# Fused gated attention and low-rank mixer on one core: where the mixer's bursts and low-rank adds stand

## The chip, the cores and the metric

The kernel runs on one core of one Trainium2 chip. The metric is the device time of one execution in microseconds (us), lower is better. Engines are named as in the profile: PE (TensorE matmuls), PEld (its weight loads), DVE (VectorE), ACT (ScalarE), POOL (GpSimd), SP (SyncE, here only a DMA queue).

## The reference

B = 8 batches, S = 3136 rows, D = 256 columns, z has 64 columns, the low rank is 32, the mixer's hidden width is 1024.

```
scores = (1/S) * z @ z^T                      # S x S, symmetric
x      = u * (max(scores, 0)**2 @ v)          # gated attention, S x D
h      = x^T @ U @ V                          # low rank along the rows: (D x S) @ (S x 32) @ (32 x S)
y      = x + h^T
out    = y + max(y @ w_ch1, 0) @ w_ch2        # mixer: D -> 1024 -> D
```

All inputs and the output are float32; the kernel computes matmuls in bfloat16 with float32 accumulation.

## The kernel before

**Tiles and turns.** A batch's 3136 rows are 25 tiles of 128 rows (the last, number 24, has 64). The tiles are worked on in the order 12, 13, ..., 24, 0, ..., 11. The place of a tile in this order, 0 to 24, is called its turn here; the code's loop `for i in range(begin, NT)` counts turns. Tiles go in pairs that share accumulators: turns (0,1), (2,3), ..., (10,11), then 12 alone, then (13,14), ..., (23,24). `open_pair` gives a pair one of two PSUM sets, each of two banks `ps` (one bank for each half of the contraction, since the two 64-row halves of PE run side by side), and the sets alternate from pair to pair. `close_pair` empties the set at the end of the pair's last turn: ACT copies bank 1 (line 385), DVE adds bank 0 (386) and multiplies with `u` (395), which gives `x_bf`.

**One turn.** `attend_steps` makes 24 steps of two matmuls (line 371), one for each source tile. About half of the steps read a block of `A` (squared scores as they were computed), the others a block of `strip`, the transpose of one row of `A`, which a DMA transpose on SP's queue (line 333) fetches some turns ahead into one of five buffers. Between the steps stand the scores of later turns and of the next batch (`score`): PE (line 298), ACT's relu (311), DVE's square (313).

**The mixer of the batch before.** While batch b attends, batch b-1 goes through the mixer. At the end of turn 0 `rank_once` computes `t1 = x^T U` (line 479, DVE 490). The rows are divided into seven chunks of four tiles (chunk 3 has three, chunk 6 two), in the order of turns. For a chunk, `low_rank` adds `h^T`: up to four matmuls (line 531) into a PSUM set, two DVE adds (545), one for each bank, into `x_bf`, and a DMA transpose to `ut` on SP's queue (504; three buffers). Then `up_steps` (563: four steps of four matmuls, `w_ch1`, relu on ACT 581, in some chunks half of the steps on DVE 571 and ACT 579) and `down_steps` (610: one step of eight matmuls for each tile, `w_ch2`; for each pair of tiles a DVE add 624 and a store, on POOL's queue, in the last batch on SP's).

**Where these stand is written out by hand.** Every engine runs its instructions in the order in which the code issues them. The dict `ahead` gives the turn at which chunk c's `low_rank` is put among the attention's steps, and `at` the step; the dict `burst_at` gives the turns after which bursts of the mixer run. A burst n merges the up steps of chunk n with the down steps of chunk n-1, with the loads of the next batch's `v` between them; burst 1 also carries DVE's copies of the next `z` (`double_z`). The next `z` is transposed on SP's queue at turns 7 and 10 (`turn_z`), and DVE extends the second part at turn 11 (`extend_z`, line 238).

**PSUM outside the accumulators.** Up steps and scores take two double banks of their own. Low-rank matmuls, down steps and some up steps take a set from `spare()`:

```
def spare():
    return sets[(opened[0] + (0 if acc else 1)) % 2]
```

With a pair open (`acc` is not empty), this is the set that the next pair will open; between a pair's close and the next open, it is the set of the pair just closed.

**The last batch.** After its turns there is no attention left to run beside its own mixer. Before its loop ends, the up steps of the last chunk of batch 6 and that batch's last down steps are kept back in `late`; they fill the time in which the last batch's `rank` sums are finished. `mix` makes chunk 0's mixer input directly (DVE, line 522), and the low-rank adds of the other chunks are placed between up and down steps. In these two chunks (`alone`) every second up step takes its PSUM from `spare()` instead of the double banks.

## Time and profile before

| | us |
|---|---|
| time, median of 3 runs (lowest to highest) | 1007.39 (1005.87 to 1008.55) |
| profiled execution: its own time | 1007.39 |
| profiled execution: its span | 1005.6 |
| PE busy in the span | 984.7 |
| ACT busy | 612.2 |
| DVE busy | 550.6 |
| POOL busy | 171.7 |

The span runs from the first to the last instruction of the program; the device time is 1.8 us longer. One batch takes about 121.9 us in the trace, and batches 1 to 6 repeat each other closely, so that a row of one of them stands for six. In the rows below the columns are the start in us, the time that the group took in us, the engine, the line, the operation, what it writes and reads, shape, count, and in square brackets the idle time before it and what ended it. A row joins instructions of one kind; a matmul's own time (0.27 us for 256 columns) is longer than the pitch at which matmuls follow each other, since they are pipelined.

### The profile page before, as it was taken

What the parts mean: (1) busy time and instruction counts of PE and PEld (TensorE: products, weight loads), DVE (VectorE), ACT (ScalarE), POOL (GpSimd) and SP (SyncE); (2) the same over time, 40 slices, a digit from 0 to 9 for tenths busy, and PEclk for the clock granted to TensorE, in tenths of its full rate; (3) what the DMA queues carried; (4) which work ended last, traced back from release to release, by engine and by line L of the source; (5) the groups of instructions that cost most, each with busy time, mean ns of one, the idle gap of its engine ahead of it and who ended that gap; (6) DMA issues with size and microseconds to landing.
All of it is one profiled execution on the core that took longest, in us unless ns stands there. A gap on an engine that the chain in (4) does not pass through costs nothing.

```text
span 1005.6 us, 30980 instructions
## 1 busy us (share of the span) xinstructions
PE 984.7 (98%) x13648; PEld 776.2 (77%) x13688; DVE 550.6 (55%) x1003; ACT 612.2 (61%) x835; POOL 171.7 (17%) x317
## 2 busy tenths in 40 slices
PE   8899999999999999999999999999999999999998
PEld 6578777787778877788777887778878788777866
DVE  6868754457444664446644566445664457542352
ACT  7877764667645776456754667556674666643154
POOL 5112112111121111121112211112111120011000
PEclk9999999999999999999999999999999999999999
DMA  9999979999898998999988997989989998568542
GB/s 190 185 188 208 172 157 172 194 178 165 152 200 166 173 166 161 182 177 173 163 176 167 183 170 146 190 172 177 177 150 188 175 180 159 132 140 155 128 98 97
DMA packets 414790, 167.94 MB, mean 167 GB/s; under 512 B 389488, under 2 KB 399408, under 8 KB 414656
## 3 DMA queue, kind: packets, MB, share of 16 engines
q1 hardware_dynamic: 385424, 99.68, 61.4%
q0 software_dynamic: 29232, 66.28, 28.4%
q8 instruction: 107, 1.75, 0.7%
q14 instruction: 27, 0.22, 0.1%
HBM read 61.88 MB, written 25.69 MB: 87 GB/s over the span
## 4 chain that ended last, share of the span: by engine, by line
PE 91%; DMA 3%; ACT 3%; DVE 2%; issue 0%; POOL 0%; DVEq 0%; ACTq 0%; POOLq 0%
PE ps L371 48%; PE ps L610 17%; PE ps L563 17%; PE ps L298 6%; ACT A L311 2%; PE ps L405 1%; DMA strip<-A 1%; PE ps L531 1%; DMA zT<-z_bf 1%; DVE x_bf L545 1%; DMA z_c<-in_z_dram 1%; DVE A L313 1%; PE ps L479 1%; PE ps L462 0%; DVE o_sb L624 0%
## 5 line engine op out<-in xcount | busy, mean ns | idle before, releaser
L311 ACT ACTIVATE A<-ps 128x832 bf16<-128x832 f32 (+9 forms) x477 | 358.9, 769 | 161.6 <-PE ps L298 153.4
L371 PE MATMUL ps<-v,A 64*128 64x256 bf16 x4988 | 341.5, 270 | 5.5 <-DVE x_bf L545 3.8
L313 DVE TENSOR_TENSOR A<-A 128x832 bf16<-128x832 bf16 (+9 forms) x477 | 244.7, 526 | 142.2 <-ACT A L311 139.2
L371 PE MATMUL ps<-v,strip 64*128 64x256 bf16 x4420 | 308.9, 270 | 2.7 <-DMA strip<-A 2.6
L371 PEld LDWEIGHTS <-A 64*128 64x128 bf16 x4988 | 246.8, 94 | 52.7 <-issue 16.2
L581 ACT ACTIVATE relu_bf<-ps 128x1024 bf16<-128x1024 f32 (+2 forms) x206 | 186.2, 911 | 139.7 <-PE ps L563 138.9
L371 PEld LDWEIGHTS <-strip 64*128 64x128 bf16 x4420 | 223.5, 94 | 38.0 <-DMA strip<-A 3.5
L624 DVE TENSOR_TENSOR o_sb<-ps,x_bf 128x512 f32<-128x512 f32 (+2 forms) x105 | 69.8, 665 | 243.5 <-PE ps L610 228.3
L610 PE MATMUL ps<-w_bf,relu_bf 128*128 128x256 bf16 (+1 forms) x1600 | 201.3, 273 | 0.6 <-DVE o_sb L624 0.5
L563 PE MATMUL ps<-ut,w_bf 128*128 128x512 bf16 (+2 forms) x856 | 196.3, 352 | 2.1
L610 PEld LDWEIGHTS <-relu_bf 128*128 128x128 bf16 (+1 forms) x1600 | 152.8, 98 | 46.2 <-issue 4.5
L298 PE MATMUL ps<-zT 64*128 64x416 bf16 (+8 forms) x812 | 133.6, 312 | 0.0
L563 PEld LDWEIGHTS <-w_bf 128*128 128x128 bf16 x896 | 85.0, 98 | 61.9 <-issue 6.7
L355 POOL DMA_DIRECT2D u_sb<-in_u_dram x96 | 53.7, 559 | 456.5 <-DVE x_bf L395 441.0
L385 ACT COPY both<-ps 128x512 f32<-128x512 f32 (+1 forms) x104 | 58.9, 566 | 73.5 <-PE ps L371 65.9
L637 POOL DMA_DIRECT2D out_dram<-o_sb x84 | 46.0, 547 | 279.9 <-DVE o_sb L624 276.5
L386 DVE TENSOR_TENSOR both<-ps,both 128x512 f32<-128x512 f32 (+1 forms) x104 | 69.2, 666 | 26.5 <-ACT both L385 25.9
L395 DVE TENSOR_TENSOR x_bf<-both,u_sb 128x512 bf16<-128x512 f32 (+1 forms) x104 | 69.8, 671 | 3.7
L545 DVE TENSOR_TENSOR x_bf<-ps,x_bf 128x512 bf16<-128x512 f32 (+1 forms) x112 | 65.4, 626 | 6.4 <-PE ps L531 6.3
L298 PEld LDWEIGHTS <-zT 64*128 64x128 bf16 x812 | 45.0, 94 | 4.2
L244 POOL DMA_DIRECT2D v<-in_v_dram x61 | 34.0, 561 | 0.9 <-DMA w_bf<-in_moe_w_ch_dram 0.8
L298 PE MATMUL ps<-relu_bf 64*128 64x416 bf16 (+9 forms) x121 | 21.9, 335 | 4.1 <-ACT A L311 3.3
(54 smaller groups left out, 206.5 us busy)
## 6 DMA issues: line engine op xcount, KB each, us to landing
u_sb<-in_u_dram POOLq DMA_DIRECT2D x96, 256.0 KB, 3.9
out_dram<-o_sb POOLq DMA_DIRECT2D x84, 256.0 KB, 3.2
v<-in_v_dram POOLq DMA_DIRECT2D x57, 192.0 KB, 4.6
strip<-A SPq DMA_TRANSPOSE x196, 5.3
out_dram<-o_sb SPq DMA_DIRECT2D x11, 256.0 KB, 2.0
z_c<-in_z_dram POOLq DMA_DIRECT2D x7, 384.0 KB, 5.8
u_sb<-in_u_dram POOLq DMA_DIRECT2D x16, 64.0 KB, 2.7
ut<-x_bf SPq DMA_TRANSPOSE x56, 3.9
```

Of the source, the lines that this page charges most:

```text
L298: mm(out=ps[:, k, :n], lhsT=zT[halves[k], j, :], rhs=zT_flat[halves[k], c : c + n], start=True, stop=True,)
L311: nc.scalar.activation(out=dst, in_=src, func=AF.Relu, scale=sc)
L313: nc.vector.tensor_tensor(out=dst, in0=dst, in1=dst, op=ALU.mult)
L371: mm(out=acc[t0][h][:, (o - t0) * D : (o - t0 + 1) * D], lhsT=w[halves[h]], rhs=v_both[b % 2][halves[h], j, :], start=start, stop=stop, **kw,)
L385: nc.scalar.copy(out=both[:, :w], in_=banks[1][:, :w])
L386: nc.vector.tensor_tensor(out=both[:, :w], in0=banks[0][:, :w], in1=both[:, :w], op=ALU.add)
L395: nc.vector.tensor_tensor(out=x_at(b, t0, n), in0=split(both[:, :w]), in1=u_sb[:, :n, :].rearrange("p t (a c) -> p t a c", c=P), op=ALU.mult,)
L545: nc.vector.tensor_tensor(out=q, in0=split(ps[h][:, : len(ks) * D]), in1=q, op=ALU.add)
L563: mm(out=ps[i][:, :w] if apart else ps[:, i, :w], lhsT=w1_bf[:, db, (hp + i) * P : (hp + i + 1) * P], rhs=uT[c][:, db, len(chunks[c]) * P ...
L581: nc.scalar.activation(out=relus[c][:, hp : hp + 2, :w], in_=ps[:, :, :w], func=AF.Relu)
L610: mm(out=ps[r, k * D : (k + 1) * D], lhsT=relus[c][:, ht, q : q + (TAIL if two else P)], rhs=w2_bf[:, ht, :], start=(ht < 1 + two), stop=( ...
L624: nc.vector.tensor_tensor(out=o_sb[:p].rearrange("p t (a c) -> p t a c", c=P), in0=split(ps[:p, k0 * D : (k + 1) * D]), in1=x_at(b, t, nk) ...
```

## The change

It moves work in the program and changes no arithmetic. In every batch the mixer runs in three bursts instead of four: chunks 0 to 2 after turn 4, 3 to 5 after turn 11, 6 and the rest after turn 16 (before: after turns 4, 8, 13 and 17). The low-rank adds of chunks 0 to 6 stand in turns 1, 2, 3, 6, 7, 10 and 14 (before: 2, 3, 6, 7, 10, 11, 14), at step 17 in the first turn of a pair and in turn 1, else at step 12 (before: 17, 13 in turn 7, else 10).

In the last batch the kept-back up steps run on without a break before the rest of `rank`, one of the two kept-back down steps stands before `mix` and one after it; chunk 0's own low-rank add moves from chunk 1's burst to chunk 0's, behind its first up step, and takes its PSUM from `spare()` instead of the set `other`; chunk 2's follows the third up step instead of the second. The last pair of tiles is added and stored as one piece of 256 KB instead of two of 128 KB.

```diff
-        apart = b == B - 1 and c == NC - 1
...
-            if apart or k == len(pair) - 1:
-                k0 = k if apart else 0
-                t, nk = pair[k0], k + 1 - k0
-                if k0 == 0:
-                    hold[1] = out_pool.tile([P, 2, D], FP32, name="o_sb")
-                o_sb = hold[1][:, k0 : k + 1, :]
+            if k == len(pair) - 1:
+                t, nk = pair[0], len(pair)
+                o_sb = out_pool.tile([P, 2, D], FP32, name="o_sb")
                 p = P if t < NF else TAIL
                 nc.vector.tensor_tensor(
-                    out=o_sb[:p].rearrange("p t (a c) -> p t a c", c=P),
-                    in0=split(ps[:p, k0 * D : (k + 1) * D]),
+                    out=o_sb[:p, :nk, :].rearrange("p t (a c) -> p t a c", c=P),
+                    in0=split(ps[:p, : nk * D]),
                     in1=x_at(b, t, nk)[:p],
                     op=ALU.add,
                 )
...
-                    store(out=rows(out[b])[:, t : t + nk, :], in_=o_sb)
+                    store(out=rows(out[b])[:, t : t + nk, :], in_=o_sb[:, :nk, :])
...
-        burst_at = {4: (0, 1), 8: (2, 3), 13: (4, 5), 17: (6, 7)}
+        burst_at = {4: (0, 1, 2), 11: (3, 4, 5), 16: (6, 7)}
...
-        ahead = dict(zip((2, 3, 6, 7, 10, 11, 14), range(NC)))
+        ahead = dict(zip((1, 2, 3, 6, 7, 10, 14), range(NC)))
...
             if b and i in ahead:
-                at = 17 if (i + (i > FIRST)) % 2 == 0 else 13 if i == 7 else 10
+                at = 17 if (i + (i > FIRST)) % 2 == 0 or i == 1 else 12
                 main.insert(at, lambda c=ahead[i]: low_rank(b - 1, c))
...
     other = sets[opened[0] % 2]
-    ups = NH // 2
     rank(b, other[0], 0, NT - 3)
-    run(late[: ups // 2])
+    run(late[: NH // 2])
     rank(b, other[0], NT - 3)
-    run(late[ups // 2 : ups])
+    run(late[NH // 2 : NH // 2 + 1])
     mix(b, 0)
+    run(late[NH // 2 + 1 :])
     low_rank(b, 1, other)
-    run(late[ups:])
     for c in range(NC + 1):
         up, down = last[c]
-        steps = _merge(up, down)
-        adds = {0: ((2, 2),), 1: ((0, 1), (3, 5))}.get(c, ((c + 2, 2),) if c + 2 < NC else ())
-        for n, at in reversed(adds):
-            steps.insert(at, lambda n=n: low_rank(b, n, other, n > 0))
-        run(steps)
+        if c + 2 < NC:
+            up.insert(3 if c == 0 else 1, lambda c=c: low_rank(b, c + 2, other))
+        if c == 0:
+            up.insert(1, lambda: low_rank(b, 0, None, False))
+        run(_merge(up, down))
```

## The prediction

> **What bounds the kernel now.** I read the page first (engine shares, chain), then the waits of PE, then the timeline around each place that the change touches. The profiled execution took 1007.39 us, which is also the median of the runs, and its span is 1005.6 us, so differences of the span add straight to the median. Of this kernel a difference below 0.3% (3.0 us) can hardly be told from none.

> The page, sections 1 and 4:

> ```profile
> PE 984.7 (98%) x13648; PEld 776.2 (77%) x13688; DVE 550.6 (55%) x1003; ACT 612.2 (61%) x835; POOL 171.7 (17%) x317
> PE 91%; DMA 3%; ACT 3%; DVE 2%; issue 0%; POOL 0%; DVEq 0%; ACTq 0%; POOLq 0%
> ```

> PE is the bound nearly everywhere: 20.9 us of its span are idle, most of them in the start-up. No matmul is added or removed, so the change can only move PE's small stalls. The waits of PE name those that lie where the change works:

> ```profile
> PE ps L371 <- DVE x_bf L545: 3.8, 7, 0.5
> PE ps L610 <- DVE o_sb L624: 0.5, 1, 0.5
> ```

> The first is one stall in each of seven batches: a low-rank add (L545) on DVE still reads the PSUM set that the next pair of output tiles wants to open. The second is the last store's, once.

> **Turn 7: a stall that shrinks.** Timeline of batch 6, around the end of turn 7:

> ```profile
> 750.37 0.69 DVE L313 TENSOR_TENSOR A<-A 128x128 bf16<-128x128 bf16 x2
> ...
> 751.71 0.49 PE L371 MATMUL ps<-v,strip 64*128 64x256 bf16 x5
> ...
> 752.00 1.01 DVE L545 TENSOR_TENSOR x_bf<-ps,x_bf 128x512 bf16<-128x512 f32 x2
> ...
> 752.74 0.72 PE L371 MATMUL ps<-v,A 64*128 64x256 bf16 x5 [0.54 <-DVE x_bf L545]
> ...
> 753.07 0.22 PEld L371 LDWEIGHTS <-A 64*128 64x128 bf16 x5 [0.24 <-issue]
> ```

> The last L371 of turn 7 starts at 751.93, pairs follow each 0.11, so turn 8 was due at 752.04; its second matmul, on the other bank, starts at 753.07, just after the second add: 1.03 us lost. After: the low-rank step stands one step earlier, and in the built program it now precedes the second score of the turn, so on DVE its adds precede that score's square. They follow the squares that end at 751.06: first add then, second 0.60 later, 0.68 long, release near 752.3. It is a 4-tile chunk instead of a 3-tile one (one matmul more, due 752.1). Stall 0.2; gain 0.8 us per batch.

> **Turn 1: a new stall.** Before, no low-rank step stands here. Timeline:

> ```profile
> 720.46 0.59 DVE L313 TENSOR_TENSOR A<-A 128x832 bf16<-128x832 bf16 x1 [0.69 <-ACT A L311]
> ...
> 721.39 0.71 PE L371 MATMUL ps<-v,A 64*128 64x256 bf16 x10
> ```

> Thirteen steps of turn 1 are done at 720.02, at 0.11 each step 17 comes at 720.45. Four matmuls take 0.22, so turn 2, due at 721.39, is now due at 721.6 (the 0.22 is only moved, from turn 11). The adds wait for the square that ends at 721.06: 720.98 to 721.66 and 721.58 to 722.26, release 722.31. Turn 1 is the second of its pair, so turn 2 opens the very set that was just used: stall 0.7 us per batch. Bounds: 0.2 (if only the first bank counted) to 1.3 (both adds after another square); I take 0.7, from the rows nearest to it. Queued behind on PE are turn 2's scores; ACT and DVE behind them shift as a whole. Turn 3's step stands two steps later than before, but DVE still runs its adds after the same square: its stall of 0.2 at turn 4 stays. Turn 14's two short adds end before turn 15 in both. Turns 2, 6 and 10 are first of their pairs: nothing opens after them.

> **Turn 16: a second new stall.** The bursts stood after turns 4, 8, 13, 17, all first of a pair: the open pair holds one set, the down steps take the other, long free. Turns 11 and 16 are second of a pair: the pair has just closed, and `spare()` gives the set it closed in. The first down step writes bank 1, which ScalarE must first copy (L385). At the end of turn 16:

> ```profile
> 804.43 0.86 ACT L311 ACTIVATE A<-ps 128x832 bf16<-128x832 f32 x1 [0.19 <-PE ps L298]
> ...
> 805.20 0.58 ACT L385 COPY both<-ps 128x512 f32<-128x512 f32 x1
> ```

> L385 stands behind a score's relu and ends at 805.78. The last L371 of the turn starts at 804.45, the burst would start 0.2 later (see below), its first up step is 256 wide (4 x 0.11), so the down step is due at 805.09 and starts at 805.83: 0.74 us. In the last batch there is no score and no up step; the copy takes 0.58 from some 0.5 after the last matmul, about 0.9. Bounds 0 to 1.3 (relu and copy whole). After turn 11 there is no score, L385 ends 0.9 after the last matmul, and the first up step (512 wide, 4 x 0.216) covers it: nothing. If that cover were gone: 0.7.

> **One burst fewer.** PE around the entry and the exit of the burst after turn 8:

> ```profile
> 755.71 0.60 PE L371 MATMUL ps<-v,strip 64*128 64x256 bf16 x7
> 756.24 1.04 PE L563 MATMUL ps<-ut,w_bf 128*128 128x512 bf16 x3
> ```
> ```profile
> 767.99 1.04 PE L610 MATMUL ps<-w_bf,relu_bf 128*128 128x256 bf16 x8
> 768.96 0.72 PE L371 MATMUL ps<-v,A 64*128 64x256 bf16 x10
> ```

> The last L371 starts at 756.04, the first L563 0.20 later, against a pitch of 0.11; the last L610 at 768.76, the next L371 0.20 later. So a burst costs 0.1 to enter and 0.1 to leave; and the change of tile shape that stood between turns 11 and 12 falls together with a burst's exit. Saved: 0.3 us per batch.
> [...]

> **Other queues.** Each low-rank step also issues one transpose on SP (L504, 1.23 us to issue, 3.9 to land). Between turns 5 and 11 there is no burst any more, while three of them, both transposes of the next z and seven strips are issued. In offsets from turn 5's start: before, from chunk 2's transpose (8.1) to the landing of turn 11's strip took 12.9 us; that gives 20.8, and turn 11 reads it at 20.8. The second z transpose then lands near 25; DVE's copy of it (L238, 0.56) and the close of turn 11's pair (L386, 0.69) stand behind it, done near 26.2; the burst wants that bank 4.3 after its start, at 26.6. So nothing, with 0 to 0.4 to spare. The v loads on POOL come a turn or a burst earlier and are not read before the next batch; the stores keep their order within a burst. z's copies stay in the second chunk. These cost nothing; the cover is whole turns of 3 us.

> **The last batch's end.** Before, chunk 0's first up step starts at 956.18. After, by the same pitches: the four late up steps run on end (953.35), rank, first down (953.77 to 954.64), mix at 954.73, its DVE add (1.23) to 956.4, second down and chunk 1's low-rank adds meanwhile; chunk 0 starts at 956.45, 0.3 later. Then its own low-rank add goes into the set that its relus use: matmuls at 957.42, adds queued behind chunk 1's (to 958.28), done at 958.88 and 959.48. The second up step was due at 957.84 and gets bank 0 at 958.93, bank 1 0.17 after it is due: 1.25 us lost. Behind it all is equal. The first down step of chunk 1's burst comes near 963.1 against 961.35: +1.75. Bounds 0.7 (chunk 1's adds already done) to 2.8 (each later relu of chunk 0 waits too).
> The last store:

> ```profile
> 1001.16 1.03 PE L610 MATMUL ps<-w_bf,relu_bf 128*128 128x256 bf16 x8 [0.51 <-DVE o_sb L624]
> 1002.24 0.42 DVE L624 TENSOR_TENSOR o_sb<-ps,x_bf 128x256 f32<-128x256 f32 x1 [1.13 <-PE ps L610]
> ```

> Its separate first half makes the last matmuls wait 0.68. After: no wait, one add of 0.69 ending 0.42 sooner, and a store of 256 KB that lands 0.2 later (2.0 against 1.8): -0.2.

> **Sum.** Per batch +0.7 (turn 1) +0.75 (turn 16) -0.8 (turn 7) -0.3 (burst) = +0.35, seven times 2.4; end +1.75 -0.2 = 1.55. Together +3.95: 1011.3 us.
> [...]

> **Rivals.** (1) *The set is free in time.* Both new stalls of the batch rest on one thing, that a score's square or relu stands ahead of the release in DVE's or ACT's queue. If the release comes 0.7 earlier (adds before 721.6, L385 before 805.1), only the batch's gains stay: 7 x (-1.1) + 1.55 = -6.2, 1001.2 us, faster. Turn 17's start, where L385 ran late and nobody waited, speaks for slack in such copies; the rows of the squares and relus ahead speak against it; 0.08. (2) *Only turn 16's does not come* (the first up step of the burst, or an earlier copy, covers it): 3.95 - 5.4 = -1.4, 1006.0; the rows of ACT speak against it; 0.15. (3) *The transposes between turns 5 and 11 run late.* Its margins are nil; 2 us late (of 17 us of transposing) stalls the burst after turn 11 by 1.6, six times: +9.6, about 1021; against it, fewer stores and v loads compete there; 0.15.

> **How the numbers follow.** The forecast has 0.62. Its own range, with the bounds (turn 1 to 1.3, end 0.7 to 2.8), is 1008 to 1015.5; 0.15 of it lies below 1010.4. So faster 0.08, same 0.15 + 0.15 = 0.30, slower 0.47 + 0.15 = 0.62. The range 1005 to 1017 takes in rival 2 and the mild part of rival 3.

> **What would show it.** In the profile after, the waits of PE should have L371 on L545 14 times (turn 2 by 0.6, turn 8 by 0.2), a new row of the down step on ACT's L385 7 times, one of about 1 us of L563 on L545 near the end, and none of the last L610 on o_sb. A wait of L371 on a strip, or of the down step on L386 behind L238, would be rival 3. No L385 row would be rival 2; without new rows I am wrong altogether.

## The result and the profile after

The changed kernel takes 1037.27 us (median, 1035.07 to 1041.62) against 1007.41 us of the kernel before, timed beside it: 1.0305 times as long, 95% interval 1.0278 to 1.0332. The forecast was 1011.3 us, at most 1017. The direction was right; the loss is 29.9 us instead of 3.9, and lies outside the range.

The profiled execution took 1036.2 us, its span is 1034.5 us (before: 1005.6). Sections 1 and 4 of its page:

```profile
PE 992.1 (96%) x13648; PEld 791.3 (76%) x13688; DVE 551.4 (53%) x1002; ACT 612.8 (59%) x835; POOL 171.5 (17%) x317
PE 84%; DMA 7%; ACT 4%; DVE 3%; issue 1%; POOL 0%; DVEq 0%; ACTq 0%; POOLq 0%
```

PE has the same matmuls. It idles 42.4 us of the span instead of 20.9, and its own work takes 7.4 us longer (4.5 of it the clock, below; the rest was not taken apart). On the chain that ended last, DMA rose from 3 to 7%. The waits of PE (releaser: us in total, times, longest; lines after the change are 608 for the down step, 619 for its add):

```profile
PE ps L371 <- DMA strip<-A: 15.0, 10, 3.1
PE ps L608 <- ACT both L385: 4.1, 7, 0.7
PE ps L608 <- DVE both L386: 4.1, 3, 2.3
...
PE ps L371 <- DVE x_bf L545: 2.3, 7, 0.3
...
PE ps L563 <- DVE x_bf L545: 1.0, 1, 1.0
```

And, of all engines, one wait of DVE, 2.6 us in the kernel before:

```profile
DVE zT L238 <- DMA zT<-z_bf: 44.4, 6, 8.1
```

The rows on L385 and L545 are those that the prediction asked for, and its price for the first (0.74 seven times) holds. The row of L371 on L545 has seven waits instead of 14, all at turn 2; turn 8's (0.17 us) is too short to show in it. The first and third rows are rival 3: attention waits for a strip that SP's transposes bring late, and the down step waits for DVE's close of the pair, which stands behind the wait for z's second transpose. The first row holds two waits of the start-up, 3.4 us together (the kernel before has one of 2.6 there), one of 0.4 in turn 4 of batch 6, and seven at one place, the end of turn 10, once in each batch: 11.2 us as the table counts them. Measured as whole gaps of PE, from when a matmul was due to when it came, these seven are 3.2, 0.9, 3.0, 1.6, 2.2, 0.6 and 0.8 us, 12.3 in all.

**How the strip comes late.** The timeline of SP in batch 6, whose turn 5 starts at 772.87 and whose turn 11 is due at 791.72:

```profile
780.75 1.21 SPq L504 DMA_TRANSPOSE ut<-x_bf  x1
782.06 1.35 SPq L333 DMA_TRANSPOSE strip<-A  x1
783.46 2.00 SPq L195 DMA_TRANSPOSE zT<-z_bf  x1
785.56 2.82 SPq L504 DMA_TRANSPOSE ut<-x_bf  x1
788.47 6.57 SPq L333 DMA_TRANSPOSE strip<-A  x3
795.13 1.46 SPq L195 DMA_TRANSPOSE zT<-z_bf  x1
```

and PE at the end of turn 10:

```profile
790.85 1.03 PE L371 MATMUL ps<-v,strip 64*128 64x256 bf16 x15
792.32 0.28 PE L371 MATMUL ps<-v,strip 64*128 64x256 bf16 x1 [0.44 <-DMA strip<-A]
```

The first of the three strips in SP's fifth row belongs to turn 11. It was issued at 788.47 and landed at 792.27; PE needed it one step before turn 11, because the last step of turn 10, the first turn of its pair, already does the last source tile for turn 11's tile. The issues of these rows stand end to end. What starts them so late is the first: chunk 3's transpose must wait for its low-rank adds in turn 6, on DVE:

```profile
779.68 1.01 DVE L545 TENSOR_TENSOR x_bf<-ps,x_bf 128x512 bf16<-128x512 f32 x2
```

They end at 780.69 and SP goes on at 780.75. Turn 10's strip stood behind chunk 3's transpose in SP's queue all that time. It takes the buffer of turn 5's strip, which was free when turn 6 began, at 776.04, so it could have gone some 6 us sooner; the second experiment shows that it does.

The kernel before issues the same transposes in the same order and at about the same offsets. Its SP rows in batch 6, whose turn 5 starts at 742.38:

```profile
750.48 1.23 SPq L504 DMA_TRANSPOSE ut<-x_bf  x1
...
755.18 1.76 SPq L504 DMA_TRANSPOSE ut<-x_bf  x1
757.03 8.02 SPq L333 DMA_TRANSPOSE strip<-A  x3
```

From turn 5's start, turn 11's strip landed there after 19.5 to 21.0 us in batches 2, 3, 4 and 6 (batches 1 and 5 have no landing in the trace) and after 17.9 in batch 7, which has no z to transpose; in the changed kernel after 19.4 to 22.0, 19.6 in batch 7. What the change moved is the time of need: 32.4 us after turn 5's start before, with the burst after turn 8 in between, and 18.8 now.

**How the second wait comes.** DVE, in batch 6, in the burst after turn 11:

```profile
798.93 0.56 DVE L238 COPY zT<-zT 128x1536 bf16<-128x1536 bf16 x1 [6.48 <-DMA zT<-z_bf]
799.40 0.68 DVE L386 TENSOR_TENSOR both<-ps,both 128x512 f32<-128x512 f32 x1
```

PE's down step starts at 800.14 after 1.42 us without work. In three batches (2, 4, 6) this cost 2.5, 0.7 and 1.4 us.

**The clock.** The granted clock was 0.50 for 3.4 us behind the strip's wait in batches 1, 3 and 5. Busy times by stretch for batch 1 (columns: stretch, its length, busy time and count of PE, PEld, DVE, ACT and POOL, granted clock, DMA share, GB/s):

```profile
158.00:161.20 3.20, 0.15 (x5) 0.01 (x2) 0.72 (x2) 0.00 (x0) 0.87 (x2) 1.00 1.19 268
161.70:165.10 3.40, 3.40 (x36) 2.46 (x34) 0.00 (x0) 0.00 (x0) 0.00 (x0) 0.50 1.12 208
165.10:168.00 2.90, 2.88 (x29) 2.06 (x26) 1.61 (x3) 1.29 (x2) 0.00 (x0) 1.00 1.09 202
```

First the wait (PE busy 0.15 of 3.20), then matmuls at half pace, then full pace. In each of the three batches 14 or 15 steps of L371 came 0.21 apart instead of 0.11: 1.5 us each.

**The sum of the differences of the span (28.9 us):** waits for the strip 12.3, halved clock 4.5, waits on L386 4.6 (each gap of PE measured whole; the table of waits, which leaves out a part of each, has 4.1), two late stalls of batches 5 and 6 1.4, the changes foreseen inside each batch (turns 1 to 11, L385, bursts) 7 x 0.8 = 5.6, the end 1.8, start-up -0.25. Two stalls of the kernel before in its batches 2 and 3 (1.4 us) are absent. Together 28.5.

### The profile page after: what moved, and what is told of

The parts are those of the page before. It is cut to its first block, busy times and chain, and to the rows that moved or that the text cites. A ratio compares the mean times of both kernels' runs of the same rounds, so it can differ in the third digit from the quotient of the medians.

```text
span 1034.5 us, 30961 instructions
## 1 busy us (share of the span) xinstructions
PE 992.1 (96%) x13648; PEld 791.3 (76%) x13688; DVE 551.4 (53%) x1002; ACT 612.8 (59%) x835; POOL 171.5 (17%) x317
## 3 DMA queue, kind: packets, MB, share of 16 engines
q8 instruction: 107, 1.75, 0.7%
## 4 chain that ended last, share of the span: by engine, by line
PE 84%; DMA 7%; ACT 4%; DVE 3%; issue 1%; POOL 0%; DVEq 0%; ACTq 0%; POOLq 0%
PE ps L371 43%; PE ps L608 16%; PE ps L563 15%; PE ps L298 6%; DMA strip<-A 5%; ACT A L311 3%; DVE x_bf L545 2%; DMA zT<-z_bf 1%; PE ps L405 1%; DVE A L313 1%; DMA z_c<-in_z_dram 1%; PE ps L531 1%; PE ps L479 1%; ACT both L385 1%; DVE both L386 0%
## 5 line engine op out<-in xcount | busy, mean ns | idle before, releaser
L311 ACT ACTIVATE A<-ps 128x832 bf16<-128x832 f32 (+9 forms) x477 | 359.3, 769 | 170.3 <-PE ps L298 162.0
L371 PE MATMUL ps<-v,A 64*128 64x256 bf16 x4988 | 346.3, 271 | 4.5 <-DVE x_bf L545 2.3
L371 PE MATMUL ps<-v,strip 64*128 64x256 bf16 x4420 | 317.1, 270 | 15.8 <-DMA strip<-A 15.0
L313 DVE TENSOR_TENSOR A<-A 128x832 bf16<-128x832 bf16 (+9 forms) x477 | 245.6, 526 | 157.3 <-ACT A L311 154.5
L371 PEld LDWEIGHTS <-A 64*128 64x128 bf16 x4988 | 260.4, 94 | 46.0 <-issue 15.7
L371 PEld LDWEIGHTS <-strip 64*128 64x128 bf16 x4420 | 235.6, 95 | 48.9 <-DMA strip<-A 18.4
L563 PE MATMUL ps<-ut,w_bf 128*128 128x512 bf16 (+2 forms) x856 | 195.0, 351 | 2.8 <-DVE x_bf L545 1.0
L619 DVE TENSOR_TENSOR o_sb<-ps,x_bf 128x512 f32<-128x512 f32 (+1 forms) x104 | 69.7, 670 | 202.0 <-PE ps L608 169.2
L298 PE MATMUL ps<-zT 64*128 64x416 bf16 (+8 forms) x812 | 139.4, 312 | 0.0
L563 PEld LDWEIGHTS <-w_bf 128*128 128x128 bf16 x896 | 85.1, 98 | 63.2 <-issue 7.6
L385 ACT COPY both<-ps 128x512 f32<-128x512 f32 (+1 forms) x104 | 58.9, 566 | 93.0 <-PE ps L371 84.4
L386 DVE TENSOR_TENSOR both<-ps,both 128x512 f32<-128x512 f32 (+1 forms) x104 | 69.2, 666 | 35.5 <-ACT both L385 35.1
L545 DVE TENSOR_TENSOR x_bf<-ps,x_bf 128x512 bf16<-128x512 f32 (+1 forms) x112 | 65.4, 626 | 8.5 <-PE ps L531 8.3
L298 PEld LDWEIGHTS <-zT 64*128 64x128 bf16 x812 | 50.7, 94 | 3.3
L238 DVE COPY zT<-zT 128x1536 bf16<-128x1536 bf16 x7 | 3.9, 559 | 44.4 <-DMA zT<-z_bf 44.4
```

The costliest lines, as they stand in the source:

```text
L298: mm(out=ps[:, k, :n], lhsT=zT[halves[k], j, :], rhs=zT_flat[halves[k], c : c + n], start=True, stop=True,)
L311: nc.scalar.activation(out=dst, in_=src, func=AF.Relu, scale=sc)
L313: nc.vector.tensor_tensor(out=dst, in0=dst, in1=dst, op=ALU.mult)
L371: mm(out=acc[t0][h][:, (o - t0) * D : (o - t0 + 1) * D], lhsT=w[halves[h]], rhs=v_both[b % 2][halves[h], j, :], start=start, stop=stop, **kw,)
L385: nc.scalar.copy(out=both[:, :w], in_=banks[1][:, :w])
L386: nc.vector.tensor_tensor(out=both[:, :w], in0=banks[0][:, :w], in1=both[:, :w], op=ALU.add)
```

## The experiments

The theory: SP's transposes of turns 5 to 11 are bunched by the in-order queue, since no burst stands there any more to give them time. Its rival: the loads and stores that moved with the bursts slow the transposes themselves. The landings above already speak against the rival, since turn 11's strip comes at about the same offset in both kernels. The first four kernels below were timed beside the kernel before at 1006.39 us, the last three beside it at 1008.63 us (1003.83 to 1012.79).

**Four bursts again.** All of the change stays but the burst turns:

```diff
-        burst_at = {4: (0, 1, 2), 11: (3, 4, 5), 16: (6, 7)}
+        burst_at = {4: (0, 1), 8: (2, 3), 13: (4, 5), 17: (6, 7)}
```

> The kernel after with the four burst turns of before (4, 8, 13, 17); low-rank adds and last batch stay as after. Queue theory (with a burst after turn 8 the transposes on SP's queue have a burst's time before turn 11 reads its strip): PE's waits for strips (15.0 us in all) and for L386 (4.1) go, the wait for L385 at turn 16 (4.1) goes, turn 1's stall of 0.7 a batch and the end's +1.8 stay: about 1009. Rival (the places of the low-rank adds alone hold the strips back): the waits for strips stay, above 1025.

Measured 1007.93 us, 1.0015 times before (1.0002 to 1.0028). The rows on L385 and L386 are gone, as is the halved clock (the mean granted clock is 1.000, in the changed kernel 0.995); the strips make 3.4 us of waits, all of them before batch 1. What remains of the change, new low-rank turns and the new end, is worth 1.5 us; the rest, some 28 us, comes only with the new burst turns.

**The two transposes later.** The bursts of the change stay; the transposes for chunks 3 and 4 are issued at the end of turn 7, behind turn 10's strip:

```diff
-                main.insert(at, lambda c=ahead[i]: low_rank(b - 1, c))
+                main.insert(at, lambda c=ahead[i]: low_rank(b - 1, c, None, c not in (3, 4)))
...
+            if b and i == 7:
+                turn_x(b - 1, 3)
+                turn_x(b - 1, 4)
```

> The kernel after, but the transposes of chunks 3 and 4 (L504) are issued on SP's queue after the strip that is issued at the end of turn 7, instead of at the low-rank adds in turns 6 and 7. Nothing else moves, the number of transfers is the same. Queue theory (strips stand idle in SP's in-order queue behind a transpose that waits for DVE's adds): the strip for turn 11 is issued near 8.5 us after turn 5's start instead of 15.5 and lands near 14, PE's waits for strips and for L386 go to about 0, the clock stays at full speed: 1036 - 23 = about 1013. Traffic theory (the DMA engines lack the throughput for what stands between turns 5 and 11): the same packets must pass, the wait only moves to another transpose: 1030 or more.

Measured 1014.64 us, 1.0099 (1.0062 to 1.0136). The same bytes move; only the order of SP's queue differs. SP in batch 6, whose turn 5 starts at 752.14:

```profile
755.51 1.42 SPq L333 DMA_TRANSPOSE strip<-A  x1
756.98 2.51 SPq L195 DMA_TRANSPOSE zT<-z_bf  x1
759.60 1.56 SPq L333 DMA_TRANSPOSE strip<-A  x1
761.20 3.45 SPq L504 DMA_TRANSPOSE ut<-x_bf  x2
```

Turn 10's strip is issued 3.4 us after turn 5's start instead of 9.2, turn 11's at 7.5 instead of 15.6. Turn 10 takes 2.95 us in every batch. The waits of PE:

```profile
PE ps L608 <- ACT both L385: 4.1, 7, 0.7
PE ps L371 <- DMA strip<-A: 2.4, 2, 1.9
...
PE ps L608 <- DVE both L386: 1.0, 3, 0.5
```

Both waits for strips lie in the start-up; none is left at the end of turn 10. So some 21 of the 30 us (1.0305 against 1.0099) hang on the place of two instructions in SP's queue.

**z's first transpose one turn later.**

```diff
-                if b and i == 7:
+                if b and i == 8:
```

> The kernel after, but the first transpose of the next z (13 blocks) is issued at turn 8 instead of turn 7, so behind the strip for turn 11. Queue theory: that strip lands about 2 us earlier in batches 1 to 6, PE's waits for strips fall from 15.0 to 3 or 4 us, with fewer halvings of the clock: 1020 to 1025. Traffic theory: nothing gained, 1033 to 1038.

Measured 1038.3 us in one run (span 1036.6): nothing gained, where the queue theory had expected 1020 to 1025. The waits of PE tell why:

```profile
PE ps L608 <- DVE both L386: 14.4, 6, 2.8
PE ps L371 <- DMA strip<-A: 6.5, 6, 2.3
```

Turn 11's strip now stands ahead of z's first transpose, and the waits at the end of turn 10 fall from 11.2 to 3.1 us (the rest of the second row is start-up), as the queue theory said. But z's second transpose lands 26.4 to 28.7 us after turn 5's start, hardly elsewhere than in the changed kernel (26.0 to 27.6). PE, less held up before the burst, now waits for it there: the wait on L386 grows from 4.1 to 14.4 us. A swap inside the bunch only moves the wait; the start of the bunch has to go forward.

**No u load in turn 8.** The load of u that turn 8 issues is left out and an older tile of u is used:

```diff
-                load_u(*after(b, o))
+                if b and o == turns(8):
+                    u_tiles[b, pair_of(after(b, o)[1])[0]] = u_tiles[b, t0]
+                else:
+                    load_u(*after(b, o))
```

> The kernel after without the load of u in turn 8 (256 KB) in batches 1 to 7; the pair of turns 10 and 11 is multiplied with the u of the pair before, which leaves that load out of the computation. Both theories have the transposes pause while it runs: the strip for turn 11 lands about 1.3 us earlier. If the pause is all that an ordinary load costs the transposes: waits for strips from 15.0 to about 6, 1024 to 1030. If loads do not hold up transposes: 1034 to 1038.

Measured 1029.24 us in one run (span 1027.5). In this kernel the down step is line 611:

```profile
PE ps L371 <- DMA strip<-A: 11.0, 8, 2.4
PE ps L611 <- DVE both L386: 4.5, 4, 1.5
```

Without this load the span is 7 us shorter; the mean granted clock is 0.996 (changed kernel 0.995). The time lies in the range that was expected if loads hold up the transposes; the waits do not (11.0 us instead of about 6), nor does the landing: turn 11's strip comes 20.0 us after turn 5's start on average, where two executions of the changed kernel have 20.6 and 20.3, and not 1.3 us sooner. In the trace of the changed kernel the transposes do slow down while the packets of this load move, for 0.7 to 2.4 us a batch: they start 0.1 to 0.5 times as many packets as in the same time just before. Of the waits at the end of turn 10, 8.6 us are left (11.2 and 10.7 in those two). So the rival has at most a small share, and one run can't say how much.

**z's copies two turns later.**

```diff
-                if i == 11:
+                if i == 13:
                     extend_z(b + 1)
```

> The changed kernel with z's copies (L238) in turn 13 instead of 11, so that DVE's close of turn 11's pair (L386) does not stand behind the wait for the second z transpose. If the two kinds of wait are independent, only the 4.1 us on L386 go: 1033 us (1031 to 1034), strip waits at the end of turn 10 stay at 12 us in all. If the wait on L386 is what upsets the order of the queues in the next batch (and so the strips too), both go and it falls below 1022.

Measured 1036.3 us in one run, a miss for either theory. Taken again beside the changed kernel:

> The changed kernel with z's copies (L238) in turn 13 instead of 11 once more, timed over several runs. Its single run before kept the whole time, 1036.3 us: the 4.1 us of waits on L386 were gone, but the strip waits at the end of turn 10 were 16 us instead of 12 and one more burst ran at the halved clock. If that was chance (the strip waits of one batch differ by 2 to 3 us from run to run), the median lies 3 to 5 us below the changed kernel of the same call, near 1032. If the time saved by DVE lets the next loads start earlier and collide with the transposes, so that one wait replaces the other, the medians agree within 2 us.

> The changed kernel itself, timed on the same chip as the run with z's copies in turn 13, for the comparison of the two: 1035 to 1041 us as before by either theory.

Measured 1036.02 us (1031.51 to 1037.62) against 1039.02 (1037.03 to 1045.14), before 1006.41. The medians differ by 3.0 us, at the edge of what chance would give. The first and second rows of PE's waits in this second profile:

```profile
PE ps L371 <- DMA strip<-A: 19.6, 9, 5.6
PE ps L608 <- ACT both L385: 4.1, 7, 0.7
```

No row on L386, as the edit intends; but the strip waits are 19.6 us, in the changed kernel timed beside it 14.1. At most 3 of the 4 us came through, and a part returned as strip waits. Most of the growth is one wait, 5.6 us in batch 4, and the single run before has one of 6.0 in batch 1. In both places the load of u in turn 8 took 7.8 us from issue to landing, in the changed kernel 4.1 to 6.4 (batches 1 to 6). What held up load and strip together stays open.

**The end alone.** The kernel before with the whole changed end of the last batch (new order of the kept-back steps, chunk 0's low-rank add behind its first up step and in the set of its relus, one last store). Its main lines:

```diff
-        adds = {0: ((2, 2),), 1: ((0, 1), (3, 5))}.get(c, ((c + 2, 2),) if c + 2 < NC else ())
...
+        if c + 2 < NC:
+            up.insert(3 if c == 0 else 1, lambda c=c: low_rank(b, c + 2, other))
+        if c == 0:
+            up.insert(1, lambda: low_rank(b, 0, None, False))
```

> The kernel before with only the changed last batch's end: chunk 0's own low-rank add in the set that its relus use, and one last store instead of two; the bursts and low-rank turns of the batches stay as before. By the two traces, where rank to the first down step of chunk 1's burst went from 11.16 to 12.92 us and the last store gave +0.08, this end costs 1.8 us by itself: 1009.2 us against 1007.4. Rival: the end is only late because the last batch of the changed kernel starts from a different state of the queues; then it costs under 0.5 us here, 1007.4 to 1007.9.

Measured 1009.31 us against 1008.63: 1.0005 (0.9987 to 1.0022). The time can't tell the theories apart, since the kernel before itself spread over 9 us there. The trace can. Its PE rows:

```profile
950.36 1.39 PE L462 MATMUL ps<-x_bf,U_bf 128*32 128x256 bf16 x44
...
959.28 2.05 PE L563 MATMUL ps<-ut,w_bf 128*128 128x512 bf16 x8 [1.04 <-DVE x_bf L545]
...
963.37 1.03 PE L608 MATMUL ps<-w_bf,relu_bf 128*128 128x256 bf16 x8
```

`rank` to the first down step of chunk 1's burst is 13.01 us; before it was 11.16 (950.19 to 961.35), in the changed kernel 12.92. The end costs 1.8 us in either surrounding, so the rival (a different state of the queues) is out.

**Turn 7 alone.** The kernel before with the low-rank step of turn 7 one step earlier:

```diff
-                at = 17 if (i + (i > FIRST)) % 2 == 0 else 13 if i == 7 else 10
+                at = 17 if (i + (i > FIRST)) % 2 == 0 else 12 if i == 7 else 10
```

> The kernel before with one thing moved: the low-rank step of turn 7 stands at step 12 instead of 13, so that on DVE its adds precede the square of the turn's second score. If the stall of 1.03 us at turn 8 comes from that order alone, as the prediction says, turn 7 shortens from 3.89 to about 3.3 us seven times: 4.1 us less, 1003.3 us, and the wait of L371 on L545 falls from 3.8 to under 1 us in all. Rival: the shorter turn of the changed kernel comes from the four-tile chunk that stands there now, not from the place; then nothing changes, 1007.4.

Measured 1000.48 us (998.77 to 1002.06) against 1008.63: 0.9914 (0.9888 to 0.9939). This is the fastest of all that ran. DVE and PE of batch 6:

```profile
746.28 1.02 DVE L545 TENSOR_TENSOR x_bf<-ps,x_bf 128x512 bf16<-128x512 f32 x2
...
747.21 0.52 DVE L313 TENSOR_TENSOR A<-A 128x704 bf16<-128x704 bf16 x1
```

The adds now stand ahead of the square of the second score. The row of L371 on L545 is gone, and turns 7 and 8 with their burst take 19.20 us instead of 20.11 in every batch: 7 x 0.91 = 6.4 us, and the spans differ by 6.2. Turn 7 itself takes 3.29 instead of 3.89, the 4.1 us expected; the rest is turn 8, which the expectation left out. The chunk in turn 7 still has three tiles here, so the rival is out.

**The change mended.** The later transposes, z's copies in turn 13, the last burst after turn 17, and the last batch's steps in the order of the kernel before (these lines are left out below; the last store stays one piece):

```diff
-        burst_at = {4: (0, 1, 2), 11: (3, 4, 5), 16: (6, 7)}
+        burst_at = {4: (0, 1, 2), 11: (3, 4, 5), 17: (6, 7)}
...
-                if i == 11:
+                if i == 13:
                     extend_z(b + 1)
...
-                main.insert(at, lambda c=ahead[i]: low_rank(b - 1, c))
+                main.insert(at, lambda c=ahead[i]: low_rank(b - 1, c, None, c not in (3, 4)))
...
+            if b and i == 7:
+                turn_x(b - 1, 3)
+                turn_x(b - 1, 4)
...
```

> The changed kernel with four things mended: the transposes for chunks 3 and 4 are issued at the end of turn 7, behind turn 10's strip, instead of with their low-rank steps; z's copies (L238) stand in turn 13 instead of 11; the last burst stands after turn 17 (first of a pair) instead of 16; the last batch's end is that of the kernel before. From the 1014.6 us that the first of these gave alone: minus 1.0 (waits on L386), minus 5.2 (waits on L385, 7 times 0.74), minus 1.8 (the end): 1006.6, and 1004 to 1008.5 with the spread of that run. The stall of turn 1 (0.7 us seven times) stays. If the loss of the changed kernel were not the sum of these waits but a matter of three bursts as such, it stays above 1011.

Measured 1005.54 us (1003.8 to 1009.49) against 1008.63: 0.9971 (0.9953 to 0.999). No waits on L385 or L386 are left, and 2.9 us for strips, all in the start-up. This kernel is 5.1 us slower than turn 7's earlier step alone, and turn 1's stall, which it still has, comes to 7 x 0.72 = 5.0. So three bursts as such cost next to nothing; nothing here shows that they gain.

## Why the prediction was wrong

**The step that failed** is in "Other queues": turn 11's strip lands at 20.8 us after turn 5's start "and turn 11 reads it at 20.8". The landing was about right (19.4 to 22.0 in the seven batches). The time of need was not: turn 11's own strip steps begin at 20.3 where nothing holds PE up (second experiment), but turn 10's last step already reads the strip, at 18.8. With two us less to spare the price is not nothing but 12.3 us. In the same paragraph, z's second transpose was put near 25 and landed between 26.0 and 27.6; of the 0.4 us to spare for L386 nothing was left, and three of six batches waited (4.6 us). That the kernel got slower, as forecast, is mostly luck: with the halved clock, 21.4 of the 28.9 us come from what the forecast put at nothing.

**Rival 3** named this mechanism, its two rows and its place, and had 0.15. Its price, 9.6 us, was for the wait on L386 alone; it too took the strip to be safe. A margin of nil in a queue whose issues stand end to end called for a higher chance and a longer range, whichever way the strip's reader had been read.

**The halved clock** (4.5 us) was not in any of the cases. No row of the kernel before shows a wait of 2 us in mid-run, and such a wait was what the rival forecast. Its start-up has one, though: PE waited 2.6 us for a strip, and the clock was halved behind it. These two stretches of the kernel before (columns as above) held the price:

```profile
46.50:49.90 3.40, 0.83 (x14) 0.44 (x11) 1.69 (x3) 0.90 (x2) 1.08 (x2) 1.00 1.23 304
49.90:53.30 3.40, 3.40 (x34) 2.30 (x32) 1.18 (x2) 1.73 (x2) 0.00 (x0) 0.51 1.00 144
```

**What held,** by its terms: turn 1's stall, +0.7 foreseen, +0.72 found (turns 1 and 2 grew by 0.94, of which 0.22 is the moved step). L385 at turn 16, +0.75 foreseen, 0.73 found; these rows of ACT and PE are batch 6's:

```profile
829.36 0.61 PE L563 MATMUL ps<-ut,w_bf 128*128 128x256 bf16 x4
829.90 0.58 ACT L385 COPY both<-ps 128x512 f32<-128x512 f32 x1
...
830.53 1.03 PE L608 MATMUL ps<-w_bf,relu_bf 128*128 128x256 bf16 x8 [0.56 <-ACT both L385]
```

Turn 7's stall, -0.8 foreseen: the gap left at turn 8 is 0.17 us where 0.2 was said, and turns 7 and 8 together with their burst, in the kernel with four bursts, are 0.64 shorter with one matmul step of 0.11 more, so -0.75. The end's +1.75: 1.76 found, in part by luck. The two parts worked out in the prediction, chunk 0 starting 0.3 later and 1.25 lost behind it, make 1.55; found are 0.45 and 1.31. (Rival 2's sum takes 5.4 where 7 x 0.75 is 5.25; its time would be 1006.1.)

**What missed by little:** the -0.3 for one burst fewer did not come (bursts without their waits 43.71 us before, 43.79 after; of this 0.1 is at the first down step of the burst after turn 11, which starts 0.32 us after the matmul ahead of it, in the burst after turn 8 of the kernel before 0.22). The last store, -0.2 foreseen, is +0.08: the last add comes sooner by 0.29, but from its issue to the end the larger store takes 3.28 us instead of 2.91. Both together move the sum by 2.9 us (7 x 0.38 and 0.28). The same sum without the failed step would have been some 1014 us.

## What to carry to other kernels

Before moving work between stretches of a kernel, write down each in-order queue's issues in the new order, with the time at which the first of them can start: one instruction that waits for a late producer holds up all behind it, and moving two of them was worth some 21 us here. Read the time of need from the first instruction that reads, not from the name of the loop turn: here the last step of the turn before reads first, some 1.5 us sooner than the turn's own strip steps. Where an engine's stall rests on the order of two instructions on another, first try that order alone: it brought 8 us in the median, 6.2 us in the spans, with no other edit.

## What the runs showed of the hardware

```profile
410.80:414.20 3.40, 0.96 (x18) 0.68 (x14) 1.53 (x3) 0.00 (x0) 1.05 (x2) 1.00 1.15 187
663.40:666.80 3.40, 1.36 (x28) 0.99 (x24) 1.03 (x2) 0.00 (x0) 1.05 (x2) 1.00 1.24 262
291.40:294.80 3.40, 1.62 (x14) 1.18 (x13) 0.68 (x2) 1.41 (x2) 0.00 (x0) 1.00 1.22 261
537.10:540.50 3.40, 1.94 (x38) 1.65 (x34) 2.33 (x4) 0.00 (x0) 1.05 (x2) 1.00 1.34 179
```

The next window was halved behind the first two, where PE was busy for 0.96 and 1.36 us of 3.4, and not behind the last two, with 1.62 and 1.94: the wait of batch 2 lies across a border of the grid. Batch 1's window, with 0.46 us (158.25 to 161.66), was followed by a halved one, as was the one with 0.83 in the start-up of the kernel before (46.50 to 49.90, above). Two windows in the start-up of the changed kernel, with 1.52 and 1.90 us (45.61 to 49.02, 49.02 to 52.44), were not. These are eight windows of two executions and no run varied the wait by itself, so a threshold was not shown.

How late a transpose comes changes from batch to batch though the program is the same: turn 11's strip took 3.8 to 6.6 us from issue to landing in the seven batches of one execution, and its wait ran from 0.6 to 3.2 us.
